# Attention weights kept compact: one transpose for two heads, and V rows of two heads stacked per layer

## The chip, the cores and the metric

The kernel runs on one core of a Trainium2 chip. The metric is the device time of one execution in microseconds (us), the median of several timed runs. The core has a matrix engine (PE, with a separate row PEld in the profile for the load of its stationary operand), a vector engine (DVE), a scalar engine (ACT), a general engine (POOL, which here issues the weight loads of the feed-forward layers and a small power operation) and SP, which issues the other transfers.

## The reference

Four layers in a row: a recurrent attention with memory (A), a gated feed-forward layer (B), and the same two once more with the same weights. The sequence has 2048 rows of width 512; A works through it in 64 segments of 32 rows, each with 8 memory rows ahead, and the memory of a segment is the output of the one before.

```python
for s in range(n_seg):
    h = concatenate([mem, x[:, s*32:(s+1)*32]], axis=1)        # 40 rows of 512
    q, k, v = (einsum('btd,dhe->bhte', h, W) for W in (Wq, Wk, Wv))   # 32 heads of 128
    scores = einsum('bhqe,bhke->bhqk', q, k) * 128 ** -0.5
    p = softmax(where(mask, scores, -1e9))                     # 40 x 40 for each head
    o = einsum('bhte,hed->btd', einsum('bhqk,bhke->bhqe', p, v), Wo)
    mem = o[:, :8]; outs.append(o[:, 8:])
...
x = x + A(layernorm(x)); x = x + B(layernorm(x))               # B: (sigmoid(x Wg) * (x Wu)) Wd, inner width 1792
x = x + A(layernorm(x)); x = x + B(layernorm(x))
```

## The kernel before

The kernel runs both attention layers as one pipeline: in step t it works on segment t of the first layer and on segment t - 6 of the second. There are 70 steps. In 58 of them both layers have a segment, and the 40 rows of each stand side by side as 80 columns (`ncol = 80`); in the first six only the first layer has one and in the last six only the second (`ncol = 40`). We call these two-layer and one-layer steps. The weights of Q, K, V and the output projection stay in SBUF throughout, loaded at the start by SP; those of the feed-forward layers are loaded again for each block of four segments by POOL.

A step goes through the 32 heads in groups of six (the last has two):

- `qk` (L738): for each head and each of Q and K four matmuls, weights stationary, 80 (or 40) moving columns. `qkcopy` evicts three heads at a time through ACT into `qku`.
- `sc` (L752): one matmul for each head, Q stationary, giving all 80 x 80 scores, of which only the two 40 x 40 blocks of a layer with itself are wanted.
- Softmax on `st`: mask added on DVE (L765, once for each layer), maximum (L770), subtraction (L772), exponential on ACT (L775), sum (L777), reciprocal (L779).
- `pmul` (L794 or, in one-layer steps, L797): the weights go to `pb` in bf16. In two-layer steps the row of a query is written twice, once times one and once times zero, by means of the mask `jm` and the small product `rz` (L784). So `pb` holds 128 columns for each head, with 80 of them used, from column 8 on, and zeros where the layers cross.
- `ptr` (L811): an ordinary matmul by the identity for each head transposes `pb` into PSUM as fp32; one copy for each group brings it to `ptsb`, on ACT or DVE.
- `pvm` (L824): one matmul for each head, the V rows `vsb` of both layers stationary (128 rows, one head's 128 columns).
- `otsb` is evicted by ACT and `wom` (L841) adds up the output projection in one bank, from which the memory rows of the next step (L854) and the output are copied.

The V rows of a step come from two places. Of each segment 24 rows are computed long before by wide V passes (`v_pass`, L596), stored in DRAM (`scr`) and loaded by SP (L698). The other rows need the new memory, or stand by it; the strips (`add_strips`, L710) compute them, 32 rows for all heads, with four column tiles of 32 beside each other. Two copies bring them to `sst`, and four SP transfers (L719) spread them to `vsb`. `vsb` is a ring of five tiles with eight heads each, four used in a step.

Feed-forward blocks (L909 to L965), layernorms with PE transposes (L565) and V passes are other work that PE does between the parts of a step. The order of each engine is fixed when the program is built: every piece is a task with an estimated duration, and a list scheduler (`Planner`) with these estimates, bank and buffer pools and 24 rounds writes out the order of all engines. A change in one task thus changes the order everywhere.

Of the kernel before, what the change touches and what calls it, by code (L numbers as in the profile page):

```python
# [9 lines left out]
BF16 = mybir.dt.bfloat16  # L10
# [6 lines left out]
P = 128  # L17
# [4 lines left out]
KOFF = 8  # L22
XS = 24
SPT = 1000
LATT = 2500.0
# [334 lines left out]
class Kern:  # L360
    def __init__(self, ctx, tc, x_in, mem0, Wq, Wk, Wv, Wo, w_gate, w_up, w_down, out, lag=6, ring=8):
# [17 lines left out]
        self.units = []  # L379
        h = 0  # L380
        while h < H:
            n = min(3, H - h)
            self.units.append((h, n))
            h += n
        self.groups = []
        u = 0
        while u < len(self.units):
            us = list(range(u, min(u + 2, len(self.units))))
            h0 = self.units[us[0]][0]
            self.groups.append((h0, sum(self.units[k][1] for k in us), us))  # L390
            u += 2
        self.HG = 6
        self.DMAT = 0
# [16 lines left out]
    def setup_tiles(self):  # L410
# [11 lines left out]
        self.maskb = c.tile([P, L], F32, name="maskb")  # L422
        self.mask1 = c.tile([L, L], F32, name="mask1")
        self.jm = c.tile([P, 2], F32, name="jm")
        self.negh = c.tile([P, 1], F32, name="negh")
        self.hT = [c.tile([P, DC, 2 * L], BF16, name=f"hT{i}") for i in range(R)]
        self.qku = [c.tile([P, 3, 2, LW], BF16, name=f"qku{i}") for i in range(3)]
        self.vsb = [c.tile([P, 1024], BF16, name=f"vsb{i}") for i in range(5)]
        self.st = [c.tile([P, HG, L], F32, name=f"st{i}") for i in range(2)]
        self.pb = [c.tile([LW, HG, P], BF16, name=f"pb{i}") for i in range(3)]  # L430
        self.mx = [c.tile([P, HG], F32, name=f"mx{i}") for i in range(2)]
        self.sm = [c.tile([P, HG], F32, name=f"sm{i}") for i in range(2)]
        self.rs = [c.tile([P, HG], F32, name=f"rs{i}") for i in range(2)]
        self.rz = [c.tile([P, 2, HG], F32, name=f"rz{i}") for i in range(2)]
        self.ptsb = [c.tile([P, HG, 2 * L], BF16, name=f"ptsb{i}") for i in range(3)]
# [6 lines left out]
        self.xn = [c.tile([P, D], BF16, name=f"xn{i}") for i in range(1)]  # L442
# [3 lines left out]
        self.xp = c.tile([P, D], BF16, name="xp")  # L446
# [17 lines left out]
    def setup_consts(self):  # L464
# [11 lines left out]
        nc.vector.memset(self.jm[:], 0.0)  # L476
        nc.vector.memset(self.jm[0:LW, 1:2], 1.0)
        nc.vector.memset(self.jm[0:L, 0:1], 1.0)
        nc.vector.memset(self.jm[0:L, 1:2], 0.0)

    def clear(self):

        nc, pl = self.nc, self.pl
        pl.add("SP", 430, lambda: nc.sync.dma_start(out=self.maskb[L:LW, :], in_=self.mask1[:]), w=["maskb"])
        for k, t_ in enumerate(self.hT):
            pl.add("DVE", 120, lambda t_=t_: nc.vector.memset(t_[:, :, L:2 * L], 0.0), w=[("hT", k, 1, q) for q in ("m", "x")])
        for k, t_ in enumerate(self.pb):
            pl.add("DVE", 400, lambda t_=t_: nc.vector.memset(t_[:], 0.0), w=[("pb", k)])
        for k, t_ in enumerate(self.vsb):
            keys = [("vs", k), ("vx", 0, k), ("vx", 1, k)]  # L490
            if k == 0:
                pl.add("DVE", 550, lambda t_=t_: nc.vector.memset(t_[:], 0.0), w=keys)
            else:
                pl.add("ACT", 960, lambda t_=t_: nc.scalar.copy(out=t_[:], in_=self.vsb[0][:]), r=[("vs", 0)], w=keys)

    def load_weights(self):
# [18 lines left out]
        for g, (h0, gsz, us) in enumerate(self.groups):  # L515
            cs = slice(h0 * P, (h0 + gsz) * P)
            nb = P * self.DC * gsz * P * 2
            for nm, sb, v in (("wq", self.wq, wq_v), ("wk", self.wk, wk_v)):
                ld(sb[:, :, cs], v[:, :, cs], nb / 300.0, [(nm, h) for h in range(h0, h0 + gsz)])
            ld(self.wo[:, h0:h0 + gsz, :], wo_v[:, h0:h0 + gsz, :], P * gsz * self.D * 2 / 300.0, [("wo", h) for h in range(h0, h0 + gsz)])  # L520
# [120 lines left out]
    def ln_x(self, b):  # L641
        if b in self.boot_x:
            xb, key = self.boot_x[b]
        else:
            xb, key = self.xp, "xp"
# [20 lines left out]
    def emit_step(self, t):  # L666
# [10 lines left out]
        nt = -(-ncol // 16) * 16  # L677
# [10 lines left out]
        def pt_all(B):  # L688
            return B[:, 0:6 * ncol].rearrange("p (h k) -> p h k", h=6)

        for j in jobs:
            s = t - j * LAG
            b, i = s // BLK, s % BLK
            row = KOFF if j == 0 else KOFF + L + MEM + SEG - XS
            for k in range(0 if j and not s else 4):
                cs = slice(k * 1024, (k + 1) * 1024)
                vu = (4 * t + k) % 5
                pl.add("SP", 430, lambda j=j, s=s, row=row, cs=cs, vu=vu: nc.sync.dma_start(  # L698
                    out=self.vsb[vu][row:row + XS, :], in_=self.scr[j][s * XS:(s + 1) * XS, cs]),
                    r=[("vd", j, b, q, kk) for q in range(3) for kk in (2 * k, 2 * k + 1)], w=[("vx", j, vu)], lat=5000.0)  # L700
        def add_strips(col, lo, key):
# [15 lines left out]
            for i in range(4):  # L717
                vu = (4 * t + i) % 5
                pl.add("SP", 430, lambda i=i, vu=vu: nc.sync.dma_start(  # L719
                    out=self.vsb[vu][KOFF + col + lo:KOFF + col + 32, :], in_=sb[32 * i + lo:32 * i + 32, :, :]),  # L720
                       r=[(sb, 0), (sb, 1)], w=[key(vu)], lat=3500.0, use=[sb])
# [377 lines left out]
```

## Time and profile before

| What | Value |
|---|---|
| median of 3 timed runs | 1858.31 us (1855.51 to 1858.92) |
| span of the profiled execution, its own time | 1854.9 us |
| granted TensorE clock, mean | 0.998 |
| PE busy | 1817.8 us (98%) |
| PEld busy | 1576.1 us (85%) |
| DVE busy | 1270.8 us (69%) |
| ACT busy | 1164.6 us (63%) |
| POOL busy | 569.4 us (31%) |

The profile is of one execution. For that execution no time is given beside its span, which runs from its first to its last instruction; the timed runs' median is 3.4 us longer. Matmuls overlap, so their durations add up to more than the time they take, and the distance from one start to the next tells more. In a row of the groups stand the line of the kernel, the engine and operation, what is written and read, the shapes (rows times columns of the stationary operand first, for PE), the count, the busy time and the mean duration in ns, and the idle time before with its cause.

### The profile page before, as it was taken

The numbers are of one execution on the slowest core, as the hardware profiler recorded it, in microseconds if no ns is written. First come the engines' busy times: TensorE is split into PE (matmuls) and PEld (weight loads), VectorE is DVE, ScalarE is ACT, GpSimd is POOL, SyncE is SP. The second block draws the span as 40 slices with busy tenths as digits, with TensorE's granted clock in tenths as the row PEclk, the third lists the DMA queues.
The fourth block names the chain that finished last, engine by engine and source line by source line (L and its number), as shares of the span: only waits on it lengthen the run. The fifth ranks groups of instructions, "written<-read, shape, count | busy, mean of one in ns | idle before, by whom it ended". The sixth has DMA issues, their size and how long they took to land.

```text
span 1854.9 us, 94296 instructions
## 1 busy us (share of the span) xinstructions
PE 1817.8 (98%) x41069; PEld 1576.1 (85%) x41282; DVE 1270.8 (69%) x4163; ACT 1164.6 (63%) x2700; POOL 569.4 (31%) x817
## 2 busy tenths in 40 slices
PE   8999999999999999999999999999999999999998
PEld 4688788889898888989888898989888898988787
DVE  4566676676677766776677667767677666767565
ACT  6655666676666666666666656666666666666554
POOL 4214022323324132423324143323324142324223
PEclk9999999999999999999999999999999999999999
DMA  9626244545546354545545364554645454545534
GB/s 359 225 68 187 58 111 134 159 130 142 167 135 172 104 169 135 158 137 141 170 130 168 97 183 134 147 148 133 175 128 167 114 169 116 153 142 155 147 98 136
DMA packets 129073, 273.81 MB, mean 148 GB/s; under 512 B 26907, under 2 KB 60451, under 8 KB 128659
## 3 DMA queue, kind: packets, MB, share of 16 engines
q0 software_dynamic: 56640, 183.09, 33.6%
q1 hardware_dynamic: 72018, 84.68, 16.1%
q8 instruction: 323, 5.29, 1.2%
q14 instruction: 92, 0.75, 0.1%
HBM read 221.85 MB, written 27.26 MB: 134 GB/s over the span
## 4 chain that ended last, share of the span: by engine, by line
PE 89%; DVE 4%; SPq 3%; issue 1%; DMA 1%; ACT 1%; POOL 0%; ACTq 0%; DVEq 0%
PE bank L738 32%; PE bank L841 16%; PE bank L941 11%; PE bank L710 7%; PE bank L596 7%; PE bank L752 5%; PE bank L811 4%; PE bank L965 4%; PE bank L824 4%; SPq L504 2%; DVE st L765 1%; PE bank L565 1%; DVE pb L794 1%; DMA wo_sb<-in_A_Wo_dram 0%; DVE mx L770 0%
## 5 line engine op out<-in xcount | busy, mean ns | idle before, releaser
L738 PE MATMUL bank<-hT,wq_sb 128*128 128x80 bf16 (+1 forms) x8960 | 621.9, 198 | 3.5 <-DVE hT L854 2.0
L738 PE MATMUL bank<-hT,wk_sb 128*128 128x80 bf16 (+1 forms) x8960 | 621.1, 198 | 0.2 <-issue 0.2
L1039 ACT CAST qku<-bank 128x480 bf16<-128x480 f32 (+3 forms) x770 | 394.2, 512 | 253.1 <-PE bank L738 211.0
L738 PEld LDWEIGHTS <-wq_sb 128*128 128x128 bf16 x8960 | 458.6, 99 | 29.2 <-issue 7.0
L738 PEld LDWEIGHTS <-wk_sb 128*128 128x128 bf16 x8960 | 450.5, 99 | 0.4 <-issue 0.4
L765 DVE TENSOR_TENSOR st<-bank,maskb 80x240 f32<-80x240 f32 (+1 forms) x732 | 269.8, 370 | 189.7 <-PE bank L752 182.2
L841 PE MATMUL bank<-otsb,wo_sb 128*128 128x80 bf16 (+1 forms) x8960 | 364.0, 198 | 4.3 <-ACT otsb L1039 1.2
L841 PEld LDWEIGHTS <-wo_sb 128*128 128x128 bf16 x8960 | 336.7, 99 | 19.1 <-issue 3.7
L933 POOL DMA_DIRECT2D wg<-in_B_w_gate_dram x217 | 164.2, 757 | 465.5 <-PE bank L941 339.7
L1039 ACT CAST otsb<-bank 128x480 bf16<-128x480 f32 (+3 forms) x420 | 201.6, 488 | 95.3 <-PE bank L824 74.7
L959 POOL DMA_DIRECT2D wd<-in_B_w_down_dram x217 | 154.3, 713 | 194.7 <-PE bank L824 64.3
L794 DVE TENSOR_TENSOR pb<-st,rz 80x480 bf16<-80x480 f32 x348 | 205.4, 591 | 3.4
L555 POOL TENSOR_TENSOR lns<-lns,negh 128x1 f32<-128x1 f32 (+1 forms) x79 | 45.2, 573 | 516.0 <-DVE lns L554 438.0
L777 DVE TENSOR_REDUCE sm<-st 80x6 f32<-80x240 f32 (+3 forms) x420 | 152.2, 364 | 63.7 <-ACT st L775 62.7
L1039 ACT CAST ptsb<-bank 128x480 bf16<-128x480 f32 (+3 forms) x298 | 151.3, 512 | 49.8 <-PE bank L811 46.1
L775 ACT ACTIVATE st<-st 80x240 f32<-80x240 f32 (+3 forms) x420 | 159.7, 382 | 31.6 <-DVE st L772 29.5
L941 PE MATMUL bank<-xnT,wg 128*128 128x128 bf16 (+2 forms) x1784 | 172.1, 219 | 2.8 <-DVE xnT L1041 1.3
L941 PE MATMUL bank<-xnT,wu 128*128 128x128 bf16 (+2 forms) x1784 | 171.1, 218 | 0.0
L752 PE MATMUL bank<-qku 128*80 128x80 bf16 (+1 forms) x2240 | 166.7, 203 | 1.2 <-issue 0.2
L934 POOL DMA_DIRECT2D wu<-in_B_w_up_dram x217 | 162.6, 749 | 1.7 <-issue 0.6
L752 PEld LDWEIGHTS <-qku 128*80 128x80 bf16 (+1 forms) x2240 | 123.2, 117 | 43.2 <-ACT sst L1039 25.9
L772 DVE TENSOR_TENSOR st<-st,mx 80x240 f32<-80x240 f32 (+3 forms) x420 | 156.0, 372 | 4.7
(99 smaller groups left out, 2461.4 us busy)
## 6 DMA issues: line engine op xcount, KB each, us to landing
wg<-in_B_w_gate_dram POOLq DMA_DIRECT2D x220, 256.0 KB, 4.5
wu<-in_B_w_up_dram POOLq DMA_DIRECT2D x220, 256.0 KB, 4.8
wd<-in_B_w_down_dram POOLq DMA_DIRECT2D x220, 256.0 KB, 5.1
vsb<-scr SPq DMA_DIRECT2D x508, 48.0 KB
vsb<-sst SPq DMA_DIRECT2D x280, 64.0 KB
scr<-vst SPq DMA_DIRECT2D x136, 96.0 KB
wq_sb<-in_A_Wq_dram SPq DMA_DIRECT2D x5, 768.0 KB
wk_sb<-in_A_Wk_dram SPq DMA_DIRECT2D x5, 768.0 KB
```

The source lines that it names most:

```text
L738: nc.tensor.matmul(o_ap, lhsT=W[:, c, h * P:(h + 1) * P], rhs=mv(c), start=(c == 0), stop=(c == DC - 1))
L752: nc.tensor.matmul(s_all(SB)[pr, uh - h0 + i, :], lhsT=qku[:, i, 0, 0:ncol], rhs=qku[:, i, 1, 0:ncol], start=True, stop=True)
L765: pl.add("DVE", dve_ns(n, True), lambda gsz=gsz, hs=hs, st=st, SB=SB, pj_=pj_, npj_=npj_, mk=mk, idx=idx: nc.vector.tensor_tensor(out=st[p ...
L772: pl.add("DVE", dve_ns(n), lambda gsz=gsz, hs=hs, st=st, mx=mx: nc.vector.tensor_tensor(out=st[pr, hs], in0=st[pr, hs], in1=mx[pr, hs].uns ...
L775: pl.add("ACT", act_ns(n), lambda hs=hs, st=st: nc.scalar.activation(out=st[pr, hs], in_=st[pr, hs], func=ACTF.Exp, scale=self.scale), r=s ...
L794: nc.vector.tensor_tensor(out=o, in0=st[pr, hs].unsqueeze(1).to_broadcast([npart, 2, gsz, L]), in1=rz[pr, :, 0:gsz].unsqueeze(3).to_broadc ...
L841: nc.tensor.matmul(WB[:, c * ncol:(c + 1) * ncol], lhsT=self.wo[:, h, c * P:(c + 1) * P], rhs=otsb[:, hl, 0:ncol], start=(h == 0 and c == ...
L933: pl.add("POOL", 760, lambda wg=wg, fs=fs: nc.gpsimd.dma_start(out=wg[:], in_=self.wgv[:, :, fs]), r=[("wo", self.H - 1)], w=[gk] + bt, la ...
L934: pl.add("POOL", 760, lambda wu=wu, fs=fs: nc.gpsimd.dma_start(out=wu[:], in_=self.wuv[:, :, fs]), r=[("wo", self.H - 1)], w=[uk] + bt, la ...
L941: nc.tensor.matmul(gu[:, 2 * i + k, 0:n], lhsT=W[:, c, i * P:(i + 1) * P], rhs=xnT[:, c, rw], start=(c == 0), stop=(c == DC - 1))
L959: pl.add("POOL", 760, lambda wd=wd, ip=ip: nc.gpsimd.dma_start(out=wd[:], in_=self.wdv[:, 2 * ip:2 * ip + 2, :]), w=[dk] + (["boot"] if se ...
L1039: nc.scalar.copy(out=dst, in_=src)
```

## The change

- Heads k and 16 + k are handled as a pair. Groups are now three pairs; the weight loads of Q, K and the output projection are split in two accordingly, one for each half of the heads.
- `pb` holds 64 columns for each head, 40 used, the rest zero. `jm`, `rz` and the doubled product go: `pmul` writes 40 columns in all steps.
- `ptr` transposes two heads at once (80 rows, 128 columns) with a PE transpose into bf16 PSUM: one for each pair.
- Two copies (`spread`), one for each head of the pair (partitions 0 to 39 and 64 to 103), bring it to `ptsb`, which has an index for the head: the weights of one head fill its own 40 partitions and its own 40 columns, and zeros stand in the other's.
- `vsb` holds, for each layer apart, the V rows of head k on partitions 0 to 39 and of head 16 + k on 64 to 103. `pvm` is one matmul for each pair and layer, 104 rows by 128 columns, 80 moving columns. The ring (`NV` = 3) has three tiles of eight pairs, two used in a step.
- The strips' rows now go to the two layers' places apart: eight SP transfers of 16 rows in a two-layer step.
- `sc` always uses 80 stationary columns, so that all 80 rows are written in one-layer steps too.
- `st` and `mx` get a third buffer, `sm` and `rs` share `mx`, the masks are bf16, `xn` gets a second buffer, `xp` is replaced by one of `xvf`.

```diff
-        self.vsb = [c.tile([P, 1024], BF16, name=f"vsb{i}") for i in range(5)]
-        self.st = [c.tile([P, HG, L], F32, name=f"st{i}") for i in range(2)]
-        self.pb = [c.tile([LW, HG, P], BF16, name=f"pb{i}") for i in range(3)]
+        self.vsb = [c.tile([P, 2, 1024], BF16, name=f"vsb{i}") for i in range(self.NV)]
+        self.st = [c.tile([P, HG, L], F32, name=f"st{i}") for i in range(3)]
+        self.pb = [c.tile([LW, HG, 64], BF16, name=f"pb{i}") for i in range(3)]
...
-                ld(sb[:, :, cs], v[:, :, cs], nb / 300.0, [(nm, h) for h in range(h0, h0 + gsz)])
+                for h0 in heads[:2]:
+                    cs = slice(h0 * P, (h0 + n) * P)
+                    ld(sb[:, :, cs], v[:, :, cs], P * self.DC * n * P * 2 / 300.0, [(nm, h) for h in range(h0, h0 + n)])
...
-            for i in range(4):
-                vu = (4 * t + i) % 5
-                pl.add("SP", 430, lambda i=i, vu=vu: nc.sync.dma_start(
-                    out=self.vsb[vu][KOFF + col + lo:KOFF + col + 32, :], in_=sb[32 * i + lo:32 * i + 32, :, :]),
-                       r=[(sb, 0), (sb, 1)], w=[key(vu)], lat=3500.0, use=[sb])
+            for i4 in (0, 2, 1, 3):
+                vh, i = halves[i4 % 2], i4 // 2
+                for j, lo, k0, nr, name in parts:
+                    if j not in jobs:
+                        continue
+                    pl.add("SP", 430, lambda i4=i4, i=i, vh=vh, j=j, lo=lo, k0=k0, nr=nr: nc.sync.dma_start(
+                        out=self.vsb[vh][64 * i + k0:64 * i + k0 + nr, j, :], in_=sb[32 * i4 + lo:32 * i4 + lo + nr, :, :]),
+                        r=[(sb, 0), (sb, 1)], w=[(name, j, vh, i)], lat=3500.0, use=[sb])
...
-                        nc.tensor.matmul(s_all(SB)[pr, uh - h0 + i, :], lhsT=qku[:, i, 0, 0:ncol], rhs=qku[:, i, 1, 0:ncol],
+                        nc.tensor.matmul(s_all(SB)[full, w0 + i, :], lhsT=qku[:, i, 0, full], rhs=qku[:, i, 1, 0:ncol],
                                          start=True, stop=True)
...
+            def pmul(gsz=gsz, hs=hs, st=st, rs=rs, pb=pb):
+                nc.vector.tensor_tensor(out=pb[pr, hs, 0:L], in0=st[pr, hs],
+                                        in1=rs[pr, 0:gsz].unsqueeze(2).to_broadcast([npart, gsz, L]), op=ALU.mult)
...
-                    for hl in range(gsz):
-                        nc.tensor.matmul(pt_all(PB)[:, hl, :], lhsT=pb[pr, hl, :], rhs=self.ident[pr, pr], start=True, stop=True)
+            def ptr(nu=nu, pb=pb, PB=PB):
+                pt = PB[:, 0:nu * LW // 2].bitcast(BF16)
+                for ul in range(nu):
+                    nc.tensor.transpose(out=pt[:, ul * LW:(ul + 1) * LW], in_=pb[full, 2 * ul:2 * ul + 2, :].rearrange("p i k -> p (i k)"),
+                                        identity=self.ident[full, full])
+            for i in (0, 1):
+                def spread(i=i, nu=nu, ptsb=ptsb, PB=PB):
+                    r = slice(64 * i, 64 * i + L)
+                    pt = PB[r, 0:nu * LW // 2].bitcast(BF16).rearrange("p (u j q) -> p u j q", u=nu, j=2)
+                    return (fview(ptsb[r, 0, i, 0:1], [(nj * LW, nu), (LW, nj), (1, L)]), pt[:, :, 0:nj, :])
+                pl.add(("ACT", "DVE"), copy_ns(nu * nj * L, True), spread, r=[PB], w=[("ptsb", pi, i)])
...
+                for ul, u in enumerate(us):
+                    for idx, j in enumerate(jobs):
+                        o = 2 * ncol * ul + L * idx
+                        nc.tensor.matmul(fview(OB[:, o:o + 1], [(ncol, 2), (1, L)]),
+                                         lhsT=self.vsb[halves[u // 8]][0:64 + L, j, (u % 8) * P:(u % 8 + 1) * P],
+                                         rhs=ptsb[0:64 + L, ul * nj + idx, :, :], start=True, stop=True)
```

## The prediction

> **What bounds the kernel now.** I read the page's busy table and slices first, then the waits of PE, then the chain, the groups kept apart by shape, and the timeline of PE.
>
> ```profile
> PE 1817.8 (98%) x41069; PEld 1576.1 (85%) x41282; DVE 1270.8 (69%) x4163; ACT 1164.6 (63%) x2700; POOL 569.4 (31%) x817
> PE   8999999999999999999999999999999999999998
> PE 89%; DVE 4%; SPq 3%; issue 1%; DMA 1%; ACT 1%; POOL 0%; ACTq 0%; DVEq 0%
> ```
>
> A busy PE alone proves little, since overlapping matmuls fill the row. So I ask what PE waits for. These are the largest entries; all of them together are 21 us of 1855.
>
> ```profile
> PE bank L538 <- DMA xo<-in_A_mem_dram: 4.3, 1, 4.3
> PE bank L565 <- DVE xn L556: 3.4, 4, 1.8
> PE bank L824 <- DMA vsb<-sst: 2.4, 3, 1.8
> PE bank L738 <- DVE hT L854: 2.0, 5, 0.6
> ```
>
> The third row is the wait that this change could enlarge. Then the price of a matmul: not its mean duration (about 200 ns, mostly pipeline), but its spacing. The chain merges runs of 72; the first row is a step with two layers (80 moving columns), the second a step with one (40).
>
> ```profile
> 182.47 2.58 PE bank L738 x72
> 77.45 1.79 PE bank L738 x72
> ```
>
> 2.58/72 is 35.8 ns, 1.79/72 is 24.9 ns. PE is issued back to back: a matmul taken away from a two-layer step is worth 36 ns, in a one-layer step 25 ns. The groups say how many there are:
>
> ```profile
> L752 PE MATMUL bank<-qku 128*80 128x80 bf16 x1856 | 141.5, 207 | 0.8 <-issue 0.2
> L824 PE MATMUL bank<-ptsb,vsb 128*128 128x80 bf16 x1856 | 120.4, 201 | 3.5 <-DMA vsb<-sst 2.4 <-DVE ptsb L1041 0.6
> L811 PE MATMUL bank<-ident,pb 80*128 80x80 bf16 x1856 | 120.3, 200 | 1.2 <-DVE pb L794 0.6
> L752 PE MATMUL bank<-qku 128*40 128x40 bf16 x384 | 25.2, 183 | 0.4
> L811 PE MATMUL bank<-ident,pb 40*128 40x40 bf16 x384 | 20.8, 179 | 1.4 <-DVE pb L797 1.4
> L824 PE MATMUL bank<-ptsb,vsb 128*128 128x40 bf16 x384 | 20.2, 181 | 0.1
> L794 DVE TENSOR_TENSOR pb<-st,rz 80x480 bf16<-80x480 f32 x290 | 187.3, 646 | 2.7
> ```
>
> 1856 is 58 two-layer steps of 32 heads, 384 is 12 one-layer steps. The timeline of a one-layer step shows a second price:
>
> ```profile
> 119.70 0.26 PE L738 MATMUL bank<-hT,wq_sb 128*128 128x40 bf16 x4
> 119.80 0.25 PE L738 MATMUL bank<-hT,wk_sb 128*128 128x40 bf16 x4
> 119.98 0.32 PE L752 MATMUL bank<-qku 128*40 128x40 bf16 x6
> 120.24 0.27 PE L738 MATMUL bank<-hT,wq_sb 128*128 128x40 bf16 x4
> ```
>
> Four QK matmuls take 0.10 us, so the scores should start at 119.90; they start at 119.98. Six of them at 25 ns should let QK go on at 120.13; it does at 120.24. So to enter a block whose stationary tile has 40 columns costs about 80 to 100 ns, and to leave it about 110. The same stands at both edges of L811 blocks with 40 contraction rows. Over all such edges in the trace the median lateness is 100 ns.
>
> **The change part by part.**
>
> *Transposes.* 32 per step become 16 (two heads side by side, 80 rows by 128 columns, still 80 moving columns). Two-layer steps: 58 x 16 x 35.8 = 33.2 us saved. One-layer steps: 12 x (32 x 25 - 16 x 35.8) = 2.7 us. They are now true PE transposes to bf16. The nearest row is the layernorm transpose, of the same kind and 128 wide:
>
> ```profile
> 48.14 0.38 PE L565 MATMUL bank<-ident,xn 128*128 128x128 bf16 x4
> ```
>
> Less one duration (224 ns) that is 3 spacings in 0.16 us, 52 ns each, what an ordinary 128-column matmul takes. The Trainium skill, "TensorE: Matmul & The Clock Gate", Part 4 PE-mode transpose, speaks against the change: some 275 ns for a 128x128 transpose in a kernel. By that, 1120 transposes would be 308 us and the kernel far slower. The row has four in 0.38 us, so I take the row.
>
> *PV.* Per layer and pair of heads: two-layer steps keep 32 matmuls of 80 columns; one-layer steps have 16 of 80 in place of 32 of 40: again 12 x 0.23 = 2.7 us saved. Contraction over 104 rows instead of 128: the trace shows no gain or loss from rows (L811 with 80 rows runs at the same duration as L824 with 128), nothing taken.
>
> *Scores.* In one-layer steps the stationary tile has 80 columns for 40. The same page, LDWEIGHTS section, gives columns/1.2, 67 ns, and its fast load only for 128 columns; by that rule 384 x (67 - 25) = 16 us lost. The trace has this 80-column load in every two-layer step, where six matmuls of L752 take 0.40 to 0.42 us, 0.207 of it one duration: about 38 ns each. I take 38: 384 x 13 = 5.0 us lost; ends 0 and 16.
>
> *Edges.* No tile is 40 rows or 40 columns wide any more. In the order of PE's instructions, before and after (the changed kernel is built, not run), changes between tile shapes fall from 419 to 142: the rest are the V strips (L710), which stay. 277 x 100 ns = 27.7 us. Half lie in the first six steps, where the V passes (L596) fill PE, half in the last six, where less other work is left. In the windows from 1700 on PE is busy 49.3 of 50, 47.9 of 50 and 50.1 of 55 us, against 296.9 of 300 us between 600 and 900: some of what is saved there will be waited away. I take 22; ends 14 and 27.7.
>
> *Vector and scalar engine.* The scaling L794 halves: 290 x (646 - 394) ns, the 394 from the 240-element L797, is 73 us; 58 small ones 5; L784 (45.9 + 8.7 us) goes. Evictions of the transposes double from 420 to 840 at half the size, in the built order 546 on ACT and 294 on DVE. ACT's 240 elements take 361 ns in the trace (x374 is 135 us), smaller ones about 0.24 (x172 is 41), for 152 before: ACT +25 us. On DVE bf16 copies from PSUM took 216 ns for 128 elements and 357 for 384, so about 280 for 240: 75 us for 59. DVE ends near 1155 us, ACT near 1190: both far under PE, so the sum counts zero. If their cover were gone it would show where PV waits for two evictions in turn: in the last small group of a step the built order has 0.93 us of PE work between transposes and PV as before, and one copy of 0.29 to 0.32 us becomes two of about 0.2. Exposed 0.1 us a step at worst: 0 to 7 us; I take 1. Three score buffers for two and two xn for one only loosen waits; xp sharing xvf touches four loads. These I count as zero.
>
> *V rows.* SP sends eight pieces from sst per step for four (512 for 284; 0.58 us median each to issue, 132 us more in all on a queue that is mostly waiting). Queued behind them are the loads of the next step's rows. The first PV now needs four pieces where it needed one, the third group all eight. From the last strip matmul to the sst copy's end took 0.64 us, a piece lands 1.9 to 3.0 us after its issue. So the first half is there after 0.64 + 3 x 0.58 + 3.0 = 5.4 us, the second after 7.7. The built PE order, with the spacings above, has 7.6 us at least and 11.9 at the median before the first PV (before: 4.9 and 5.6), and 10.0 and 15.6 before the third group. The strips now stand ahead of their step's QK. Covered: zero. Three half buffers with two used per step: the second half's buffer is free once three PV groups of the step before are done, half a step early.
>
> *Start.* The Q and K weights come in 768-byte runs for 1536. In the packet records 512 B took 29 ns, 1024 B 49, 1536 B 66; 768 B about 39. So 10240 x 39 / 16 = 25.0 us for 21.1 at a time when the queues are full: the last weights, on which step 0 ends (the chain there is SP's weight loads, then wo_sb), come up to 3.8 us later. V passes fill part of it: I take 2, ends 0 and 4.
>
> *Sum.* -33.2 - 2.7 - 2.7 + 5.0 - 22 + 1 + 2 = -52.6 us on the profiled execution's 1854.9: 1802.3. The median of the timed runs is 1858.31, 3.4 us above that span, so 1805.7. About 0.2% (4 us) can be told from no change here.
>
> **The rivals.**
>
> *Only the counts pay.* One-layer steps turn out bound by their recurrence, so of the edges a quarter (7 us) is left, scores run at 67 ns, start and evictions cost their upper ends: -38.6 + 16 - 7 + 4 + 7 = -18.6, so 1840; with scores at 38 ns 1829. For it: the idle of the last windows. Against: half of the edges lie in steps that the V passes fill.
>
> *V rows late (slower).* Every step's third group waits for the eighth piece. The gain of 53 us is 0.75 us per step over 70 steps; the wait passes that when the eighth piece lands 15.6 + 0.75 = 16.4 us after the strips, which is 0.64 + 7 x 1.8 + 3.0: 1.8 us of issue per piece decides (1.0 at the shortest distance in the order). At 2.0 us per piece the wait is 2.0 us a step, 140 us in all: 1946. For it: single pieces took up to 1.8 us, and SP issues in order. Against: the median of 0.58, and only 2.4 us of such waits now.
>
> *Evictions bind (same or slower).* Where PE waits for the second copy in each of 420 groups, 0.13 us of it eats the gain; a whole 0.3 us would give 1806 + 126 = 1932. For it: two copies of one bank in turn. Against: ACT at 63%, DVE falling, and PV waits for ptsb of 0.6 us in all.
>
> **How the numbers follow.** The forecast 0.78; only the counts 0.12; V rows late 0.05; evictions 0.05, of which 0.02 near no change. Faster 0.90, same 0.02, slower 0.08. The forecast's own bounds are 1792 (all edges, no losses: -38.6 - 27.7) to 1822 (-38.6 + 5 - 14 + 4 + 7, all at their worse ends but the scores); waits that merely shrink or grow by a few us with a new order put 4 us more below. The first rival reaches from 1829 to 1840. Range 1788 to 1838.
>
> **What would show it.** PE's records fall by 1312 less what is missing; chain spacing stays 35.8 ns; the transposes' spacing is near 36; no late start at score blocks of one-layer steps; PE's wait for vsb stays under 10 us. Wrong if PE falls well under 97% busy, if PV waits for sst in most steps, or if the transposes stand over 60 ns apart.

## The result and the profile after

| | before | after |
|---|---|---|
| median of 4 timed runs each | 1856.91 us (1854.64 to 1858.92) | 1827.34 us (1825.91 to 1830.84) |
| span of the profiled execution | 1854.9 us | 1825.3 us |

The changed kernel takes 1.6% less: ratio 0.9843, 95% interval 0.9829 to 0.9857. That is 29.6 us where the sum said 52.6. (The median of before has a fourth run here, 1854.64 us, and so lies 1.4 us under the one that the prediction started from.) The granted TensorE clock is 0.998 in both profiles. The busy table, PE's slices and the chain of the page:

```profile
PE 1776.6 (97%) x39783; PEld 1533.6 (84%) x39970; DVE 1162.9 (64%) x3927; ACT 1194.2 (65%) x3005; POOL 569.9 (31%) x817
PE   7999999999999999999999999999999999999998
PE 81%; DVE 9%; ACT 4%; SPq 3%; issue 2%; DMA 1%; POOLq 0%; ACTq 0%; DVEq 0%
```

The busy times of DVE and ACT are what was forecast (about 1155 and 1190). Yet the chain, which was 89% PE, 4% DVE and 1% ACT, now has 9% and 4% of them: a chain that leaves PE more often, with DVE at 64% and ACT at 65%. PE's waits say the same (in a row: microseconds in total, number of waits, the longest):

```profile
PE bank L826 <- ACT otsb L1024: 8.1, 30, 0.6
PE bank L808 <- ACT ptsb L1024: 4.1, 15, 0.6
PE bank L526 <- DMA xo<-in_A_mem_dram: 3.9, 1, 3.9
PE bank L553 <- DVE xn L544: 3.8, 2, 3.5
PE bank L730 <- DMA wk_sb<-in_A_Wk_dram: 3.2, 4, 1.5
PE bank L787 <- DVE pb L775: 1.9, 5, 1.0
```

The two largest are evictions on ACT. Before, the same two places had:

```profile
PE bank L841 <- ACT otsb L1039: 1.2, 3, 0.7
PE bank L824 <- DVE ptsb L1041: 0.6, 3, 0.2
```

No row for `vsb` waiting on `sst` is left. The groups, kept apart by shape:

```profile
L744 PE MATMUL bank<-qku 128*80 128x80 bf16 x1856 | 132.0, 206 | 1.4 <-ACT qku L1024 1.1
L808 PE MATMUL bank<-ptsb,vsb 104*128 104x80 bf16 x2048 | 143.8, 199 | 5.5 <-ACT ptsb L1024 4.1 <-DMA vsb<-scr 0.2
L787 PE MATMUL bank<-ident,pb 80*128 80x80 bf16 x1120 | 104.3, 200 | 2.8 <-DVE pb L775 1.9
L744 PE MATMUL bank<-qku 128*80 128x40 bf16 x384 | 28.2, 193 | 0.8 <-ACT qku L1024 0.5 <-issue 0.2
L775 DVE TENSOR_TENSOR pb<-st,mx 80x240 bf16<-80x240 f32 x290 | 114.9, 396 | 1.2
L1024 ACT COPY ptsb<-bank 40x240 bf16<-40x240 bf16 x374 | 130.7, 352 | 33.3 <-PE bank L787 29.1 <-DVE ptsb L1026 0.8
L1026 DVE COPY ptsb<-bank 40x240 bf16<-40x240 bf16 x206 | 56.9, 277 | 10.6 <-PE bank L787 7.8 <-ACT ptsb L1024 0.2
```

The copies of `ptsb` that they replace were, before:

```profile
L1039 ACT CAST ptsb<-bank 128x480 bf16<-128x480 f32 x233 | 130.4, 563 | 38.0 <-PE bank L811 35.5 <-DVE lns L554 1.1
L1041 DVE CAST ptsb<-bank 128x480 bf16<-128x480 f32 x57 | 37.2, 653 | 6.9 <-PE bank L824 4.4 <-PE bank L811 0.8
```

PE has the counts that were forecast (2240 transposes are 1120 and the built program has 1312 matmuls fewer), and the copies have the durations that were taken: 352 ns on ACT for 361, 277 on DVE for 280. So the durations do not tell what went wrong. Spacing on PE, from the chain and the timeline of PE:

```profile
239.31 2.58 PE bank L730 x72
```

```profile
119.28 0.25 PE L730 MATMUL bank<-hT,wq_sb 128*128 128x40 bf16 x4
119.38 0.25 PE L730 MATMUL bank<-hT,wk_sb 128*128 128x40 bf16 x4
119.48 0.39 PE L744 MATMUL bank<-qku 128*80 128x40 bf16 x6
...
1004.83 0.27 PE L787 MATMUL bank<-ident,pb 80*128 80x80 bf16 x3
1004.94 1.89 PE L584 MATMUL bank<-wv_sb,xvl 128*128 128x512 bf16 x8
```

2.58/72 is 35.8 ns again. In the one-layer step the scores start right at 119.48, with no late start, and six take 0.39, less one of 0.193: 39 ns each. Three transposes hold PE from 1004.83 to 1004.94, 37 ns each, nowhere near the 275 of the rule that the prediction weighed.

To see where the rest went I laid every matmul of the built order at a spacing and took the sum from the time. The spacing is the planner's formula in the kernel, columns/2.4 + 2.3 ns, with 25 ns as its least value. It gives 35.6 and 25 where the chain shows 35.8 and 24.9, and 216 for 512 columns, where the last row above has (1.89 - 0.38)/7 = 0.216 us. Four strip matmuls beside each other count once. What remains, the *excess*, is waits, edges, the wider scores' 5 us and lateness too small for the list of waits. The sum of the spacings goes from 1756.2 to 1717.6, that is -38.6 us, as the forecast's matmul terms; this is arithmetic on the counts, which the spacings in the trace bear out. The excess goes from 98.7 to 107.7 where it was to fall by 14 (steps are counted from 0 to 69, and a stretch ends with the last output-projection matmul of its last step):

| stretch | excess before | excess after |
|---|---|---|
| start to the end of step 0 | 11.0 | 12.4 |
| steps 1 to 5 (one-layer) | 14.0 | 10.7 |
| two-layer steps, 6 to 62 | 42.3 | 60.6 |
| steps 63 to 68 (one-layer from 64 on) | 17.0 | 10.0 |
| step 69 and what follows | 6.3 | 6.5 |

The rest, 8.0 and 7.5 us, lies before the first matmul and after the last. The second and fourth row, called the one-layer steps below, win, as the edges were to bring: 31.0 us are 20.7. The two-layer steps, where nothing was to be lost, lose 18.3 us.

### The profile page after: what moved, and what is told of

It is laid out like the page before. It is cut to its first block, busy times and chain, and to the rows that moved or that the text cites. A ratio compares the mean times of both kernels' runs of the same rounds, so it can differ in the third digit from the quotient of the medians.

```text
span 1825.3 us, 92117 instructions
## 1 busy us (share of the span) xinstructions
PE 1776.6 (97%) x39783; PEld 1533.6 (84%) x39970; DVE 1162.9 (64%) x3927; ACT 1194.2 (65%) x3005; POOL 569.9 (31%) x817
## 4 chain that ended last, share of the span: by engine, by line
PE 81%; DVE 9%; ACT 4%; SPq 3%; issue 2%; DMA 1%; POOLq 0%; ACTq 0%; DVEq 0%
PE bank L730 28%; PE bank L826 16%; PE bank L926 10%; PE bank L698 7%; PE bank L584 6%; PE bank L950 4%; PE bank L744 4%; PE bank L808 3%; DVE st L758 3%; SPq L485 3%; PE bank L787 2%; ACT ptsb L1024 1%; DVE pb L775 1%; DVE mx L763 1%; ACT qku L1024 1%
## 5 line engine op out<-in xcount | busy, mean ns | idle before, releaser
L826 PE MATMUL bank<-otsb,wo_sb 128*128 128x80 bf16 (+1 forms) x8960 | 370.2, 198 | 9.6 <-ACT otsb L1024 8.1
L826 PEld LDWEIGHTS <-wo_sb 128*128 128x128 bf16 x8960 | 345.4, 99 | 35.0 <-issue 11.3
L1024 ACT COPY ptsb<-bank 40x240 bf16<-40x240 bf16 (+3 forms) x546 | 170.8, 315 | 53.0 <-PE bank L787 46.0
L770 DVE TENSOR_REDUCE mx<-st 80x6 f32<-80x240 f32 (+3 forms) x420 | 151.6, 364 | 50.7 <-ACT st L768 47.2
L744 PE MATMUL bank<-qku 128*80 128x80 bf16 (+1 forms) x2240 | 160.2, 204 | 2.2 <-ACT qku L1024 1.6
L775 DVE TENSOR_TENSOR pb<-st,mx 80x240 bf16<-80x240 f32 (+3 forms) x420 | 154.9, 369 | 4.0
L763 DVE TENSOR_REDUCE mx<-st 80x6 f32<-80x240 f32 (+3 forms) x420 | 153.0, 364 | 5.4
```

The source lines that it names most:

```text
L744: nc.tensor.matmul(s_all(SB)[full, w0 + i, :], lhsT=qku[:, i, 0, full], rhs=qku[:, i, 1, 0:ncol], start=True, stop=True)
L763: pl.add("DVE", dve_ns(n), lambda hs=hs, st=st, mx=mx: nc.vector.tensor_reduce(out=mx[pr, hs], in_=st[pr, hs], axis=AX.X, op=ALU.max), r=s ...
L775: nc.vector.tensor_tensor(out=pb[pr, hs, 0:L], in0=st[pr, hs], in1=rs[pr, 0:gsz].unsqueeze(2).to_broadcast([npart, gsz, L]), op=ALU.mult)
L826: nc.tensor.matmul(WB[:, c * ncol:(c + 1) * ncol], lhsT=self.wo[:, h, c * P:(c + 1) * P], rhs=otsb[:, hl, 0:ncol], start=(h == 0 and c == ...
L1024: nc.scalar.copy(out=dst, in_=src)
```

## The experiments

**Where is the loss: the second copy left out.** The order of every engine is that of the changed kernel.

```diff
             for i in (0, 1):
                 def spread(i=i, nu=nu, ptsb=ptsb, PB=PB):
-                    r = slice(64 * i, 64 * i + L)
+                    if i:
+                        return None
+                    r = slice(0, 64 + L)
```

> The changed kernel in the same order of all engines, but of the two copies of a transposed group the second is left out and the first takes all 104 partitions, starting at partition 0; the second head's weights are thus not applied. Theory A: with 420 copies in place of 840, none of them starting at partition 64, ACT is on time: PE's waits for ACT otsb and ACT ptsb (8.1 and 4.1 us in the trace) fall under 2 us together, and of the 18 us of new PE waits in two-layer steps 12 to 18 go: 1806 to 1815. Theory B: the waits lie in the order, 1821 to 1827.

Measured: 1803.78 us (1801.42 to 1806.13), ratio to the kernel before 0.9713 (0.9699 to 0.9728). Against the changed kernel's 1827.34, leaving the second copy out is worth 23.6 us. The excess in two-layer steps falls to 40.1, just under the 42.3 of before, and that of the one-layer steps from 20.7 to 15.5. The page's busy table and chain of this run:

```profile
PE 1771.8 (98%) x39970; PEld 1527.4 (85%) x39970; DVE 1117.3 (62%) x3787; ACT 1113.6 (62%) x2725; POOL 569.9 (32%) x817
PE 92%; SPq 3%; ACT 2%; DVE 2%; DMA 1%; issue 1%; POOLq 0%; ACTq 0%; DVEq 0%
```

ACT goes from 65% to 62% busy and DVE from 64% to 62%, and with that the chain from 81% to 92% PE.

**Why is a second copy of 352 ns so dear?** The trace says how far apart instructions start. The trace does not hold an instruction's first partition, but the built order does, and both have the same instructions of ACT and DVE. On ACT, a copy of 240 columns takes some 352 ns in every case, but where the next instruction follows at once, it starts (medians):

| first partition of the copy, of the next instruction | ACT, ns to the next start | DVE |
|---|---|---|
| 0, 0 | 268 | 190 |
| 64, 64 | 259 | (too few) |
| 0, 64 | 364 | 288 |
| 64, 0 | 379 | 317 |

While the first partition stays, an instruction on ACT overlaps the one before by 84 to 93 ns; when it changes, the next starts only after the end. A pair of spread copies on ACT is 364 + 379 = 743 ns. The single fp32 copy of 480 columns that it replaces was 455 to the next start, for a duration of 563. The timeline of ACT, first of the changed kernel and then of the next experiment, shows it in the length of a merged pair (start, us, line, shapes):

```profile
1129.90 0.73 ACT L1024 COPY ptsb<-bank 40x240 bf16<-40x240 bf16 x2
1130.65 0.56 ACT L1024 CAST qku<-bank 128x480 bf16<-128x480 f32 x1
```

```profile
1122.82 0.62 ACT L1024 COPY ptsb<-bank 104x240 bf16<-104x240 bf16 x2
1123.32 0.40 ACT L931 ACTIVATE th<-bank 128x256 f32<-128x256 f32 x1
```

Above, 0.73 less one duration of 0.35 is 0.38 between the two starts, and `qku`, which starts at partition 0, comes 0.75 after the pair began. Below, with both copies from partition 0, 0.62 less 0.37 is 0.25, and the next instruction comes after 0.50.

**The change of partition taken away, both copies kept.** The order is again that of the changed kernel.

```diff
-                    r = slice(64 * i, 64 * i + L)
+                    r = slice(0, 64 + L)
```

> Both copies of a group's spread cover 104 partitions from partition 0, without a mask (the zeros of the other head are left out); number of copies and order of every engine as in the changed kernel. Theory A1, what costs is that an instruction whose first partition differs from the one before does not overlap it: distance of such a copy on ScalarE back to 255 ns from 364 to 379, a pair 510 instead of 743 ns, and about half of the 23.5 us that leaving the second copy out gave: 1812 to 1818 us. Theory A2, the second copy as such, whatever its length, with its extra wait: no gain, 1825 to 1828 us.

Measured: 1807.15 us (1806.28 to 1810.37), ratio 0.9731 (0.9717 to 0.9746). The kernel leaves out the zeros of the other head; as many copies of about the same duration as in the changed kernel stay (366 for 352 ns on ACT, 272 for 277 on DVE), and 20.2 of the 23.6 us are back. That is more than theory A1 expected and excludes A2. The excess in two-layer steps is 44.1. The chain, ACT's copies and the largest wait of the changed kernel, which shrinks:

```profile
PE 92%; SPq 3%; ACT 2%; DVE 1%; issue 1%; DMA 1%; POOLq 0%; ACTq 0%
L1024 ACT COPY ptsb<-bank 104x240 bf16<-104x240 bf16 x374 | 115.0, 366 | 30.9 <-PE bank L787 28.7
PE bank L826 <- ACT otsb L1024: 5.0, 19, 0.5
```

**The same, with the zeros written by a mask.** Both copies cover 104 rows from partition 0 and multiply by a column of ones and zeros; the function and the order are kept.

```diff
-                    r = slice(64 * i, 64 * i + L)
+                    r = slice(0, 64 + L)
...
-                    nc.scalar.copy(out=dst, in_=src)
+                    nc.scalar.activation(out=dst, in_=src, func=ACTF.Copy, scale=self.half[r, i:i + 1])
```

(on DVE a `tensor_scalar` by the same column)

> The changed kernel in the same order, both copies kept, but each reads and writes partitions 0 to 103 and multiplies by a column of ones and zeros for its half, so that no instruction starts at partition 64. Theory A1 (what costs is the change of the first partition from one instruction to the next: 110 to 125 ns on ACT and DVE in the trace): distance from a 240-element copy to the next instruction on ACT falls from 364 to 379 ns to about 255, on DVE from 278 to 317 to about 190 to 330 (its multiplication may be slower), and most of the new PE waits go: 1808 to 1816. Theory A2 (what costs is the doubled number of copies, not where they start): distance stays near 360, time 1823 to 1830. Theory B: 1823 to 1830 although the distance falls.

Measured: 1825.87 us (1824.67 to 1827.3), ratio 0.9832 (0.9818 to 0.9847): nothing gained that can be told from the changed kernel's 1827.34.

```profile
L1028 ACT ACTIVATE ptsb<-bank,half 104x240 bf16<-104x240 bf16 x374 | 151.0, 462 | 28.5 <-PE bank L791 27.9 <-DVE ptsb L1030 0.2
L1030 DVE TENSOR_SCALAR ptsb<-bank,half 104x240 bf16<-104x240 bf16 x206 | 63.1, 333 | 12.1 <-PE bank L791 11.0
```

The masked instruction takes 462 ns on ACT for the 366 of the plain copy of 104 rows, and its distance is 354 ns; on DVE the distance is 251, about half way from 303 (the mean of the changed kernel) to 190. Distance and time are those that theory A2 named, but the preceding run excludes A2: here the change of partition is gone, and the mask has taken the time that this gave back on ACT. So the loss follows the time on the engines, not the partition as such. That DVE was relieved of half its part without a gain speaks for ACT. A masked copy also ends later, and the run does not separate that from the time that ACT is held. The Trainium skill, "ScalarE: Activation LUTs", What ACT_TABLE_LOAD costs, gives 93 ns for a column operand and 93 for the overlap of two instructions in a row; the runs show 96 (for an ACTIVATE with the column in place of a plain copy) and, for the overlap, 84 to 114, and this only where the first partition stays.

**What were the edges worth?** Narrow tiles back in the one-layer steps of the changed kernel, and full tiles in those of the kernel before, each in its kernel's own order.

```diff
# changed kernel, narrow tiles back
-  matmul(s_all(SB)[full, w0 + i, :], lhsT=qku[:, i, 0, full], ...)
+  matmul(s_all(SB)[pr, w0 + i, :], lhsT=qku[:, i, 0, 0:ncol], ...)
-  transpose(out=pt[:, ul * LW:(ul + 1) * LW], in_=pb[full, ...], identity=self.ident[full, full])
+  transpose(out=pt[:, ul * LW:ul * LW + ncol], in_=pb[pr, ...], identity=self.ident[pr, pr])
# kernel before, full tiles
-  matmul(s_all(SB)[pr, uh - h0 + i, :], lhsT=qku[:, i, 0, 0:ncol], ...)
+  matmul(s_all(SB)[0:LW, uh - h0 + i, :], lhsT=qku[:, i, 0, 0:LW], ...)
-  matmul(pt_all(PB)[:, hl, :], lhsT=pb[pr, hl, :], rhs=self.ident[pr, pr], ...)
+  matmul(pt_all(PB)[:, hl, :], lhsT=pb[0:LW, hl, :], rhs=self.ident[0:LW, pr], ...)
```

> The changed kernel in the same order, with scores and transposes of the one-layer steps on 40 columns and 40 rows again. If the edges between tile shapes cost 100 ns each and PE is what bounds those steps: 27.7 us more, less 5 for the narrower scores and 2 for the transposes, so 1827 + 20 = 1847. If those steps are bound by the chain from memory to memory and by the loads at the start: some 8 us more, 1835. If edges cost nothing: 1820.

Measured: 1839.84 us (1839.51 to 1841.22), 12.5 us slower than the changed kernel and between the first two cases of the expectation. Narrow tiles also save the 5.0 us of the wider scores and 2.0 of the transposes (192 of 36 ns at 25), so the edges themselves cost 19.5 us. In its timeline they are as they were before:

```profile
122.38 0.25 PE L730 MATMUL bank<-hT,wk_sb 128*128 128x40 bf16 x4
122.56 0.32 PE L744 MATMUL bank<-qku 128*40 128x40 bf16 x6
...
124.66 0.32 PE L744 MATMUL bank<-qku 128*40 128x40 bf16 x6
124.91 0.27 PE L730 MATMUL bank<-hT,wq_sb 128*128 128x40 bf16 x4
```

QK could be done at 122.48 and the scores start at 122.56.

> The kernel before, with its score matmuls and its transposes in the steps of one layer given full 80-column tiles (zeroed operands), so that TensorE changes its tile shape only for the 32-column strips; every engine's order is as before. Theory E1, the 277 edges that go are worth their whole 100 ns: about 27.7 less some 5 us for the wider matmuls, 1834 us. Theory E2, in the steps of one layer much of an edge lies in time in which TensorE would have waited for VectorE or ScalarE: about 12 to 15 us, as the changed kernel with narrow tiles lost 12.5; 1842 to 1846 us.

Measured: 1847.86 us (1841.57 to 1850.25), ratio 0.9936 (0.9915 to 0.9956): 9.6 us gained, somewhat less even than theory E2 said. With the 5.0 us of the wider scores the edges were worth 14.6 here. The excess of the one-layer steps alone falls by 12.7, with the 5.0 of the scores 17.7 for the edges; narrow tiles in the changed kernel raised it by 14.4 (20.7 to 35.1), with the 5.0 again 19.4. So within those steps the two kernels nearly agree. The rest is lost elsewhere: here the excess of the start, the two-layer steps and the tail rises by 1.7, 2.7 and 1.9. At the start the added clearing of the operands may be the reason; why the other two lose with the same work in the same order stays open.

**Is it luck of the order?** The planner's order reacts to any number. One cost was nudged, and in another kernel the planner was told the distances above as the cost of a copy.

```diff
# nudged
-  pl.add("DVE", 110, lambda ...: nc.vector.reciprocal(...)
+  pl.add("DVE", 112, lambda ...: nc.vector.reciprocal(...)
# costs told
-  pl.add(("ACT", "DVE"), copy_ns(nu * nj * L, True), spread, ...)
+  pl.add(("ACT", "DVE"), {"ACT": nu * nj * L * 0.833 + 172.0, "DVE": nu * nj * L / 1.92 + 178.0}, spread, ...)
```

> The changed kernel with the planner's cost of the reciprocal at 112 instead of 110 ns: the same instructions in another order. It sizes what an order is worth by itself. Theory A: within 4 us of 1827, and the 12.5 us that the run with measured copy costs lost are of those costs. Theory O: 8 us or more off, either way, with the two-layer steps' waits for otsb changed by as much.

> The changed kernel, 1827 us, with one edit: the scheduler's estimate of the two copies of a transposed group is raised to what the trace showed as their distance to the next instruction (ACT 240 elements 372 ns where it had 252, DVE 303 where it had 198). The instructions are the same ones, in a new order. Theory A (ACT runs behind the written order, since these copies cost more than planned, and PE waits for otsb, ptsb and qku): the 14 us that PE waits in such places fall by half or more, time 1812 to 1820. Theory B (the new form makes the order itself worse, with less PE work between the parts of a group, whatever the copies cost): no gain, 1823 to 1832. The start and the one-layer steps stay as they are in both.

Measured: nudged 1829.56 us (1828.61 to 1831.18), within 4 us as theory A said. Costs told 1839.81 (1839.0 to 1840.81), 12.5 us slower than the changed kernel and outside both theories. The excess of the two-layer steps is 64.2 and 72.8, for 60.6. So all three orders of the changed kernel have the loss, and it is not one order's accident. A small nudge moved the time by 2 us in the one trial, but an order can be 12 us worse with nearly the same work (16 of the large copies went from ACT to DVE). Why the told costs led to a worse order was not found; that a mean cost does not describe a copy whose cost depends on its neighbours is a guess.

**Versions that keep the function and move the copies.** Each has an order of its own. First, the copies held to an engine by their partition, so that ACT never changes; then two others:

```diff
# pinned
-  pl.add(("ACT", "DVE"), copy_ns(nu * nj * L, True), spread, ...)
+  pl.add("DVE" if i else "ACT", copy_ns(nu * nj * L, True), spread, ...)
# only the upper copy held to DVE
+  pl.add("DVE" if i else ("ACT", "DVE"), copy_ns(nu * nj * L, True), spread, ...)
# both copies on ACT
+  pl.add("ACT", copy_ns(nu * nj * L, True), spread, ...)
```

> The whole function is kept, in a new order: the copy of a group that begins at partition 0 always runs on ScalarE, the one that begins at partition 64 always on VectorE, so that ScalarE never changes its first partition and VectorE pays every change. Theory A1 (the changes of first partition on ScalarE are what costs): distance of the copy on ScalarE back to 250 to 255 ns, PE's waits for otsb under 5 us, most of the 20 us that the copies from partition 0 gave: 1808 to 1816 us. Rival D (VectorE's chain of the softmax is as near to its limit as ScalarE is): the changes, some 100 ns into and 127 ns out of each copy, now lie in front of the softmax's steps, PE waits for pb, and the time is 1825 to 1840 us.

> As the pinned run, but the copy from partition 0 may run on either engine as the planner likes; only the copy from partition 64 is held to VectorE. Theory A1: as the pinned run within 5 us, 1806 to 1816 us. Rival D: 1822 to 1840 us, with PE's waits for pb and ptsb on VectorE.

Measured: 1868.99 us (1867.97 to 1872.82) and 1858.12 (1854.46 to 1859.9); the first is slower than the kernel before, ratio 1.007 (1.0055 to 1.0085), the second as fast as it, 1.0005 (0.9995 to 1.0014). Rival D was right in kind and too small. PE's waits and the chain of the pinned run:

```profile
PE bank L787 <- DVE pb L775: 18.0, 42, 0.8
PE bank L826 <- ACT otsb L1024: 6.2, 21, 0.8
PE bank L808 <- DVE ptsb L1026: 4.3, 9, 2.1
```

```profile
PE 65%; DVE 26%; ACT 3%; SPq 2%; issue 2%; DMA 1%; ACTq 0%; DVEq 0%
```

ACT's copies are back at 256 ns, as they were to be. But of DVE's 290 large copies 271 now have 317 ns to the next start, they lie among the steps of the softmax, and PE waits for `pb`: 18.0 us for 1.9. DVE is 65% busy in this run. In the second, the planner gave DVE 378 of the 580 large copies, and PE waits 9.5 us for `ptsb` on DVE and 7.8 for `pb`.

> The whole function is kept, in a new order: both copies of every group run on ScalarE, none on VectorE. VectorE loses 206 copies of some 300 ns (62 us), ScalarE gains 206 of some 371 ns (76 us). Theory S (ScalarE's occupancy is what sets the loss): more waits for otsb and ptsb, 1840 to 1860 us. Theory D (as the two pinned runs suggest, it is VectorE's softmax that may not be loaded further, and ScalarE has room): waits for pb go and the time is 1810 to 1826 us.

Measured: 1853.83 us (1851.38 to 1856.54), ratio 0.9977 (0.9968 to 0.9986): theory S. DVE leaves the chain, ACT takes its place, and the waits for evictions grow by half:

```profile
PE 85%; ACT 9%; SPq 3%; issue 2%; DMA 1%; DVE 0%; ACTq 0%
```

```profile
PE bank L826 <- ACT otsb L1024: 12.0, 43, 0.5
PE bank L808 <- ACT ptsb L1024: 6.4, 24, 0.7
```

So neither engine has room: 72 us less busy time on DVE and 81 more on ACT lose 26.5 us, and the opposite (56 more on DVE and 41 less on ACT, pinned) loses 41.7. Both are well over the 12.5 us that an order by itself was seen to make. The runs side by side, the large copies of `ptsb` (count by ns to the next start) and the excess of the two-layer steps:

| kernel | on ACT | on DVE | excess |
|---|---|---|---|
| second copy left out | 183 x 255 = 47 us | 107 x 190 = 20 us | 40.1 |
| before | 233 x 455 = 106 | 57 x 574 = 33 | 42.3 |
| both from partition 0 | 374 x 252 = 94 | 206 x 190 = 39 | 44.1 |
| masked | 374 x 354 = 132 | 206 x 251 = 52 | 56.8 |
| changed kernel | 374 x 371 = 139 | 206 x 303 = 62 | 60.6 |
| both on ACT | 580 x 371 = 215 | 0 | 82.0 |
| pinned | 290 x 256 = 74 | 290 x 317 = 92 | 94.5 |

Up to about 100 us on ACT and 40 on DVE the excess stays within 4 us (40.1 to 44.1); the changed kernel lies past that on both. The rows are not enough to divide its loss between the two engines: only the masked run, where ACT's share is all but unchanged and DVE's is down by 10 us, with no gain in time, speaks for ACT.

**The zeros in V.** One copy, and V tiles of which each holds one head's rows and zeros in the other's place; two matmuls of 40 columns for one of 80.

```diff
-        self.NV = 3
+        self.NV = 2
-        self.vsb = [c.tile([P, 2, 1024], ...
+        self.vsb = [c.tile([P, 2, 2, 1024], ...
...
+    for i in (0, 1):
+        nc.tensor.matmul(OB[:, o + i * ncol:o + i * ncol + L],
+                         lhsT=self.vsb[halves[u // 8]][0:64 + L, i, j, (u % 8) * P:(u % 8 + 1) * P],
+                         rhs=ptsb[0:64 + L, ul * nj + idx, :], start=True, stop=True)
```

> The whole function is kept. One compact copy per group from partition 0 over 104 rows; the zeros move to V (each V tile has one half per head with the other head's rows zero), so the weighted sum is two matmuls of 40 columns instead of one of 80. For room the V tiles are 2 instead of 3, the down-weight buffers 2 instead of 3 and the gate buffer 1 instead of 2; the planner makes a new order. Theory A (the second copy's time on ScalarE and VectorE is what was lost): near the run with the second copy left out, plus 2.7 us for the matmuls and a few for the buffers: 1806 to 1816 us. Theory O (the luck of an order moves these kernels by 10 us and more): anything between 1805 and 1835 us, with waits for otsb as in the changed kernel.

Measured: 1836.08 us (1833.98 to 1837.44), above what either theory named. The expectation's 2.7 us for the matmuls was a slip (it is the price in one-layer steps alone): all 2048 become two, 2048 x (2 x 25 - 35.6) is 29 us, and the sum of the spacings does go from 1717.6 to 1747.0. Less those 29.4, the run stands at 1806.7, where theory A put it; its excess in two-layer steps is 37.6. So the second copy costs less than the matmuls that replace it.

**The weighted sum's copy freed from ACT.**

```diff
-  pl.add("ACT", act_ns(gsz * ncol, True), lambda ...: (otsb[:, hs, 0:ncol], ...
+  pl.add(("ACT", "DVE"), copy_ns(gsz * ncol), lambda ...: (otsb[:, hs, 0:ncol], ...
```

> The changed kernel, whole function, in a new order: the copy of the weighted sum (otsb), until now on ScalarE alone, may run on ScalarE or VectorE as the planner finds them free; 88 of 420 go to VectorE. Theory S: waits for otsb, 8.1 us in the changed kernel, fall by half and the stretch of two-layer steps gives 5 to 10 us: 1815 to 1823 us. Theory D: VectorE's chain gets later by as much or more: 1827 to 1840 us.

Measured: 1826.47 us (1824.36 to 1827.15), which can't be told from the changed kernel. The waits for `otsb` do fall, from 8.1 to 2.7 us (and 0.6 for those on DVE), but the excess of the two-layer steps only from 60.6 to 57.1: the largest row of the list of waits was not where most of the loss lay. No version that keeps the function clearly beat the changed kernel.

## Why the prediction was right in its direction and off in its size

| term of the sum | taken | measured |
|---|---|---|
| transposes and PV | -38.6 | -38.6, by the built counts at spacings that the trace bears out |
| wider scores | +5.0 | 39 ns each, as taken |
| edges | -22 | -14.6 and -19.5, in the two kernels |
| vector and scalar engine | +1 | +20.2 and +23.6, by the two runs that relieve them |
| V rows | 0 | 0: the wait for `vsb` is 0.2 us |
| start | +2 | +1.4 |

With 19.5 for the edges (the value in the changed kernel) and 22 for the copies (between the two runs) the sum is -38.6 + 5.0 - 19.5 + 22 + 1.4 = -29.7, against 29.6 measured. With the ends of both terms it lies between -23.2 and -31.5, so the terms account for the time, but the close fit is a choice of middle values. The run with the second copy left out stands near the sum without its eviction term: 1805.7 - 1 = 1804.7, and it took 1803.8. Part of that is luck: the edges brought less than the 22 taken, and that run has less copying than the kernel before (ACT is busy 1113.6 us for 1164.6).

**The step that failed** is "both far under PE, so the sum counts zero", with the "0 to 7" that bounded it. It was wrong in three ways. First, a copy was costed by its duration in the groups; what a queue pays is the distance to the next start, and this depends on the neighbour's first partition. By duration a pair is twice 352 for one of 563; by distance it is 743 for 455 on ACT, which the rows of before could not show, since there every instruction on ACT starts at partition 0. Second, the share of busy time (63 and 69%) was read as room. The runs with copies moved either way show that there was none to spare on either engine; that their idle third is cut into short pieces by the recurrence, each engine working in its written order, would explain it but was not measured. Third, exposure was looked for only in the small group at the end of a step. It was 0.32 us for each of the 57 steps measured, mostly in pieces too short for the list of waits, which in these steps grows only from 8.5 to 13.7 us. How the loss divides between the two engines stays open.

The prediction weighed two sections of one page of the Trainium skill against its rows, rightly held to the rows, and passed over another page. "VectorE: DVE Perf Modes", Two Vector instructions with no wait between them, states as a model that an instruction that reads or writes a memory in another group of 32 partitions than the last one did there starts only when all earlier ones are done. The DVE column above agrees (288 and 317 ns for 190, duration 277). By that rule, read beside `slice(64 * i, ...)`, the copies on DVE would have been priced without overlap. The page has no price for it; by this trace it is 206 copies at 303 ns for 190, 23 us more time on DVE. For ACT the runs show the same behaviour.

**The rivals.** "Only the counts pay" gives 1829 to 1840, and with scores at 38 ns its sum is -29.6 us, the measured number. That is luck, for two of its terms are wrong and cancel: it has 7 us for the edges, which paid 14.6 to 19.5, and 7 for the evictions, which cost 20 to 24. "V rows late" did not come: the pieces from `sst` took 0.59 us at the median to issue, as assumed. "Evictions bind" named the right part, at 20 to 24 us over 420 groups or 0.05 us a group, under the 0.13 from which it would have eaten the gain. Its place was not quite right: the wait for the second copy itself (`ptsb`, 4.1 us) is smaller than that for `otsb` on the same engine, 8.1 us, which falls to 5.0 where the copies of `ptsb` get shorter.

**The signs it named.** 1312 matmuls fewer, 35.8 ns, transposes near 36, no late scores in one-layer steps, `vsb` under 10 us: all came (PE is 97% busy), and all concern PE or transfers. None was named that would have shown a loss on ACT or DVE beyond PV's waits.

## What to carry to other kernels

Cost an eviction by the distance to the next start on its engine, not by its duration, and ask at which partition its neighbours start: here a copy that began at partition 64 among instructions at 0 gave up the overlap on both sides. Two small copies for one large one are then no even trade, and an in-order engine at 65% busy in a recurrent pipeline may have no room at all; try it by leaving the work out, in the same order of instructions. Before a cheap-looking eviction is traded for matmuls, price the matmuls: at 25 to 36 ns each, 2048 of them cost more than the copies.

## What the runs showed of the hardware that was not expected

- On ACT a change of the first partition between two instructions removes their overlap: 364 to 379 ns to the next start for 259 to 268 (240 bf16 columns from PSUM), 264 to 279 for 156 (120 columns). The two directions differ by 15 ns. On DVE it is 288 and 317 for 190. The copies change their partition in what they read and in what they write, and no run separates the two.
- A copy that reads and writes 104 partitions is nearly as fast as one of 40: 361 to 366 ns for 352 on ACT, 272 to 274 for 277 on DVE, and no longer to the next start.
- A copy with a column operand as its scale takes 96 ns more on ACT (462 for 366) and 61 on DVE (333 for 272), and about as much more to the next start (354 for 252, 251 for 190). It is also another instruction, ACTIVATE and TENSOR_SCALAR for COPY, so the operand alone is not shown to be the cause.
